# A cross-attention block feeding a maxout network on one core: scores and softmax with the tokens along the free dimension, VectorE's 32x32 transposes for the sums, one run of zero matmuls at the start, and the first tokens loaded in two halves of the heads

## The chip, the core and the metric

The kernel runs on one core of a Trainium2 chip. The metric is the device time of one execution in microseconds (us). The engines run in parallel, each with its own list of instructions in a fixed order, and meet through semaphores: PE (TensorE: matmuls and their weight loads), DVE (VectorE), ACT (ScalarE), POOL (GpSimd), and SP, which here only issues DMAs. PE writes to PSUM, which has eight banks; DVE and ACT copy out of PSUM into SBUF. POOL here works from SBUF to SBUF and issues the DMAs that change f32 into bf16 on the way.

## What is computed

```python
# attention, x: (8,8,512,64), state: (8,8,32,64)
scores = scale * x @ state^T          # (8,8,512,32)
a = softmax over the 32 states;       xread = a @ state
scores2 = scale * state @ x^T         # (8,8,32,512), the same numbers transposed
a2 = softmax over the 512 tokens;     sread = a2 @ x
y = concat([xread, sread], tokens)    # 8 batches of 512 + 32 rows, 8 heads x 64 = 512 columns
# maxout network on 4352 rows
h = max(y @ w1, y @ w2, y @ w3)       # 512 -> 768
out = h @ w_out                       # 768 -> 512
```

Both softmaxes come from one matrix of exponentials, summed over the states in one and over the tokens in the other.

## The kernel before, in words

Work is cut by batch. For a batch b the kernel does the following; the short names are those of its written schedule.

- `lx`, `pm`: load x[b] as bf16 by a POOL DMA, and permute it into `xn` (tokens on partitions). Batch 0 comes instead as f32 in one SP DMA (`x32`, 1 MB), behind the DMA of the state (`st32`, 512 KB).
- `xT` or `xb`: transpose `xn` into `xT`, by PE (16 transposes of 128x128 and two copies out of PSUM) for batches 0 to 2, by one SP DMA for the later ones.
- `S` (two halves of 256 tokens): scores `ps` with the tokens on the partitions (8 matmuls per half, each with 128x128 of `xT` as weights and 64 columns of the block-diagonal state `sbd` moving), the exponential `e` (ACT), the sum over the 32 states `den` and its reciprocal `rden` (DVE), and the product `a` (POOL).
- `aT` or `ab`: transpose `a` into `aT` (heads x states on the partitions), by PE for batches 0 to 2, by one SP DMA for the others.
- `R`: the state reads. 8 matmuls with `ones` sum `e` over the tokens, 16 matmuls multiply `xn` with `e`; DVE takes a 128x128 reciprocal (L279) and two products (L282) into `AT`.
- `M` (six units per batch): `M_sb`, the state of the batch already multiplied with the three weight matrices `W`. Eight matmuls per unit run side by side in tiles of 64 rows x 32 columns (`pm`); two copies of 128x384 bring them out.
- `u` (18 per batch, as block m = 0..5 and matrix i = 0..2): `pw`, two matmuls of 512 columns, `M_sb` against `aT`. Matrix 0 is copied out by ACT (`t`, L300), matrix 1 and 2 are folded in by DVE maxima against PSUM (L304, L306) into `ht`. The state rows of all batches form a ninth group that multiplies `AT` with `W` directly.
- `o` (8 per batch): `po`, `ht` against `wout`, three matmuls of 512 columns each; every second one ends with a copy by ACT and the output DMA from SP.

The order of the work is written out by hand: every engine runs its instructions in the order in which these strings name them. `OPENING` covers batch 0 and 1 and the attention of batch 2. `PERIOD` is used six times (the u of group g beside the o of the group before), `LAST` once. The groups run 0 to 6, then the state rows, then batch 7. `idle n` issues n matmuls of zeros into a bank that is not read; the opening has 9, 9 and 8 of them. POOL loads the weights in four pieces (`lw`, in columns of W), three DMAs each.

Where the profile says L106 or L109 that is the helper for all matmuls or transposes, and L101 or L103 the helper for all copies by ACT or by DVE and POOL; they are told apart by tile names.

Of the kernel before, what the change touches and what calls it, by code (L numbers as in the profile page):

```python
# [8 lines left out]
F32 = mybir.dt.float32  # L9
# [17 lines left out]

OPENING = """
id, idle 9, sel, idle 9, pm 0 0 a, pm 0 1 v, lx 1, xT 0 0 v, lw 2 4, pm 1 1 v, pm 1 0 v,
xT 0 1 a, idle 8, lw 1 2, lw 0 1, S 0 0 g, S 0 1 g, xT 1 1 a, xT 1 0 a, R 0, lw 4 6,  # L30
S 1 1 g, aT 0 0 a, M 0 2 va, aT 0 1 v, S 1 0 g, M 0 3 aa, M 1 3 av, M 1 2 aa, M 2 1 vv,
u 0 3 0, u 0 3 1, M 0 1 aa, u 0 2 0, M 1 1 va, aT 1 - v, u 0 2 1, M 0 0 aa, R 1, u 0 1 0,
lx 3, u 1 1 0, u 0 2 2, u 0 0 0, u 1 1 1, M 0 5 aa, M 0 4 aa, lx 2, u 0 1 1, u 0 3 2, lo,
u 1 3 0, u 0 0 1, u 0 5 0, M 1 0 va, pm 2 - g, u 1 3 1, u 1 1 2, u 0 4 0, M 2 2 aa,
u 1 3 2, lx 4, u 0 5 1, pm 3 - g, u 1 0 0, M 2 5 aa, M 1 5 aa, xb 3, u 0 1 2, u 0 5 2,
u 1 2 0, xT 2 1 v, u 0 4 1, u 0 0 2, u 1 5 0, u 0 4 2, xT 2 0 a, u 1 0 1, S 2 1 g,
o 0 0 0 v, M 1 4 aa, M 2 3 aa, o 0 0 1 v, u 1 2 1, o 0 1 0 v, S 2 0 g, u 1 5 1, u 1 2 2,
o 0 1 1 a, o 0 2 0 v, o 0 2 1 a, M 2 0 aa, M 2 4 aa, aT 2 - v, u 1 4 0, u 1 0 2, u 1 5 2,
o 0 3 0 v, o 0 3 1 a, u 1 4 1, u 1 4 2, R 2
# [4 lines left out]
u u u P L S S o o u M M m o u u o u u u o u u o X u M m m R u o u u u o u u  # L44
"""
LAST = """
u u u u u u M M u u u S u o u o u u M u u R u u M o u o S M L o M P o o X o
# [4 lines left out]
def kernel(  # L52
# [9 lines left out]
):  # L62

# [22 lines left out]
    xnp = ctx.enter_context(tc.tile_pool(name="xnp", bufs=3))  # L86
    att2 = ctx.enter_context(tc.tile_pool(name="att2", bufs=2))
    tmpp = ctx.enter_context(tc.tile_pool(name="tmpp", bufs=4))
# [19 lines left out]
    def tr(out_ap, in_ap):  # L108
# [6 lines left out]

    st32 = res.tile([128, Ns // 2, D], F32, name="st32")
    nc.sync.dma_start(
        out=st32.rearrange("p n d -> p (n d)"),
        in_=state.rearrange("b h (q n) d -> (b h q) (n d)", q=2))

    x32 = res.tile([128, H, J, D], F32, name="x32")
    nc.sync.dma_start(out=x32.rearrange("p h j d -> p h (j d)"),
                      in_=x[0].rearrange("h (p j) d -> p h (j d)", j=J))
    zeros = const.tile([128, 512], BF16, name="zeros")
    nc.vector.memset(zeros, 0.0)  # L125
    sbd = res.tile([128, B, HP, 2, Ns], BF16, name="sbd")
# [14 lines left out]
    def load_w(m0, m1):  # L141
        c = slice(m0 * 128, m1 * 128)
        for i in range(3):
            nc.gpsimd.dma_start(out=W[:, i, :, c], in_=w_v[i][:, :, c])  # L144
# [307 lines left out]
```

The softmax here doesn't subtract the row's maximum and nothing guards it: scores larger than these inputs give would overflow.

## Time and profile before

| what | value |
|---|---|
| median of 13 runs | 160.4 us (159.81 to 160.61) |
| the profiled execution's own time | 160.61 us |
| its span (first to last instruction) | 158.8 us |
| PE busy | 149.8 us, 94% |
| DVE, ACT, POOL busy | 112.0 (71%), 94.6 (60%), 44.2 (28%) us |
| last matmul ends | 155.40 us |
| one repeat of `PERIOD` (from one `S S` to the next) | 15.66 us (49.74 to 65.41, 65.41 to 81.07, ...) |

A line of groups names a source line, an engine, an operation and its output and inputs; then how often it ran, the busy time that the group covered, and the mean duration of one in nanoseconds. Matmuls overlap in the pipeline, so a mean duration of 380 ns does not mean that one can start only every 380 ns: the chain of waits shows two `pw` matmuls in 0.43 us. The chain of waits is followed back from the last instruction, and each of its lines gives a start, a length and what ran or was waited for.

### The profile page before, as it was taken

The page shows a single profiled execution, that of the slowest core. Times are in us where ns is not written, and L with a number is a line of the kernel's source. Part 1 is how long each engine was busy: PE and PEld are TensorE (multiplying, and loading weights), DVE is VectorE, ACT ScalarE, POOL GpSimd, SP SyncE. Part 2 cuts the span into 40 slices and gives each one's busy share as a digit, 9 for nine tenths or more (in the row PEclk, how much of TensorE's full clock was granted, in tenths as well). Part 3 has the DMA queues.
Part 4 walks back from the last instruction along what each step waited for, and adds up shares of the span by engine and source line. Part 5 has one row for each costly group of instructions (what it writes and reads, how often), then busy time and mean ns, then how long its engine had stood idle before and what let it go on. Part 6 is the DMA issues. An engine that isn't in the chain of part 4 may idle for free.

```text
span 158.8 us, 3558 instructions
## 1 busy us (share of the span) xinstructions
PE 149.8 (94%) x1387; PEld 75.3 (47%) x1404; DVE 112.0 (71%) x200; ACT 94.6 (60%) x188; POOL 44.2 (28%) x48
## 2 busy tenths in 40 slices
PE   7858899999999999999999999999999999999991
PEld 2337453344445445444444444454444467754450
DVE  3356999978669879867896889688968834478601
ACT  3557979668464956595658566855676533344440
POOL 8915990092550740092009000400040000000000
PEclk9999999999999999999999999999999999999999
DMA  4999999979649589729981708270306033030253
GB/s 148 290 194 190 149 176 155 191 111 196 109 114 261 114 202 132 214 50 170 163 232 40 198 0 210 60 198 2 136 20 179 4 132 132 0 132 4 66 187 143
DMA packets 34400, 21.46 MB, mean 135 GB/s; under 512 B 19536, under 2 KB 31824, under 8 KB 34384
## 3 DMA queue, kind: packets, MB, share of 16 engines
q0 software_dynamic: 14400, 6.82, 34.0%
q1 hardware_dynamic: 19840, 14.29, 32.6%
q8 instruction: 11, 0.18, 0.4%
q10 hardware_dynamic: 144, 0.13, 0.2%
q14 instruction: 5, 0.04, 0.1%
HBM read 15.20 MB, written 8.91 MB: 152 GB/s over the span
## 4 chain that ended last, share of the span: by engine, by line
PE 85%; DMA 5%; DVE 3%; ACT 2%; issue 1%; POOL 1%; SPq 0%; DVEq 0%; POOLq 0%
PE pw L106 43%; PE po L106 28%; PE pm L106 6%; DMA x<-in_x_dram 5%; PE pr L106 4%; PE ps L106 2%; PE px L109 1%; DVE M_sb L103 1%; POOL a L246 1%; PE pz L106 1%; PE pa L109 1%; DVE den L242 1%; ACT M_sb L101 1%; ACT xn L101 1%; ACT e L238 0%
## 5 line engine op out<-in xcount | busy, mean ns | idle before, releaser
L106 PE MATMUL pw<-aT,M_sb 128*128 128x512 bf16 x288 | 71.9, 380 | 0.0
L106 PE MATMUL po<-wout,ht 128*128 128x512 bf16 (+1 forms) x194 | 51.1, 373 | 0.8
L304 DVE TENSOR_TENSOR t<-t,pw 128x512 bf16<-128x512 bf16 (+1 forms) x54 | 35.4, 655 | 19.1 <-PE pw L106 8.9
L300 ACT CAST t<-pw 128x512 bf16<-128x512 f32 (+1 forms) x54 | 30.6, 569 | 29.3 <-PE pw L106 28.9
L106 PEld LDWEIGHTS <-M_sb 128*128 128x128 bf16 x288 | 26.9, 98 | 30.9 <-issue 0.8
L306 DVE TENSOR_TENSOR ht<-t,pw 128x512 bf16<-128x512 bf16 (+1 forms) x54 | 35.2, 657 | 6.8 <-PE pw L106 3.0
L246 POOL TENSOR_TENSOR a<-e,rden 128x512 bf16<-128x512 bf16 x16 | 16.4, 1041 | 59.6 <-ACT e L238 36.3
L101 ACT CAST M_sb<-pm 128x384 bf16<-128x384 f32 x75 | 31.1, 509 | 1.3 <-PE pm L106 0.6
L101 ACT COPY o<-po 128x512 f32<-128x512 f32 x32 | 18.7, 585 | 18.6 <-PE po L106 16.1
L106 PEld LDWEIGHTS <-ht 128*128 128x128 bf16 x210 | 19.6, 98 | 21.3 <-issue 1.9
L103 POOL COPY xn<-x 128x2048 bf16<-128x2048 bf16 x6 | 11.3, 1887 | 8.2 <-DMA x<-in_x_dram 8.2
L106 PE MATMUL pm<-W,sbd 64*32 64x384 bf16 x384 | 12.4, 327 | 0.1
L242 DVE TENSOR_REDUCE den<-e 128x16 f32<-128x512 bf16 x16 | 10.6, 661 | 2.2 <-ACT e L238 2.1
L238 ACT ACTIVATE e<-ps 128x512 bf16<-128x512 f32 x16 | 9.0, 598 | 4.6 <-PE ps L106 4.6
L103 DVE CAST M_sb<-pm 128x384 bf16<-128x384 f32 x21 | 10.6, 534 | 0.0
L144 POOL DMA_DIRECT2D W<-in_moe_w_dram x12 | 9.0, 766 | 4.0 <-DMA x<-in_x_dram 3.3
L106 PE MATMUL pw<-AT,W 128*128 128x256 bf16 x72 | 9.2, 273 | 0.1
L106 PEld LDWEIGHTS <-sbd 64*32 64x32 bf16 x384 | 4.4, 90 | 9.3 <-issue 8.7
L106 PE MATMUL pz<-zeros 128*128 128x512 bf16 x25 | 7.5, 457 | 1.2 <-DVE zeros L125 1.2
L106 PEld LDWEIGHTS <-W 128*128 128x128 bf16 x72 | 7.0, 98 | 2.5
L279 DVE RECIPROCAL rd<-pr 128x128 f32<-128x128 f32 x8 | 7.6, 944 | 0.0
L153 POOL DMA_DIRECT2D x<-in_x_dram x7 | 6.6, 943 | 0.1
(39 smaller groups left out, 66.8 us busy)
## 6 DMA issues: line engine op xcount, KB each, us to landing
out_dram<-o SPq DMA_DIRECT2D x14, 512.0 KB, 2.9
x<-in_x_dram POOLq DMA_DIRECT2D x7, 512.0 KB, 7.5
W<-in_moe_w_dram POOLq DMA_DIRECT2D x6, 256.0 KB, 7.8
x<-in_x_dram SPq DMA_DIRECT2D x1, 1024.0 KB, 7.4
W<-in_moe_w_dram POOLq DMA_DIRECT2D x6, 128.0 KB, 10.8
wout<-in_moe_w_out_dram POOLq DMA_DIRECT2D x1, 768.0 KB, 12.8
out_dram<-o SPq DMA_DIRECT2D x3, 256.0 KB, 2.1
st<-in_state_dram SPq DMA_DIRECT2D x1, 512.0 KB, 3.7
```

What stands on the lines that cost most here:

```text
L101: nc.scalar.copy(out=o, in_=i)
L103: ENG[eng].tensor_copy(out=o, in_=i)
L106: nc.tensor.matmul(out_ap, lhsT, rhs, start=start, stop=stop, tile_position=pos)
L144: nc.gpsimd.dma_start(out=W[:, i, :, c], in_=w_v[i][:, :, c])
L153: nc.gpsimd.dma_start(out=x_sb[b].rearrange("p h j d -> p h (j d)"), in_=x[b].rearrange("h (p j) d -> p h (j d)", j=J))
L238: nc.scalar.activation(out=e.rearrange("p r n -> p (r n)"), in_=ps.rearrange("p j a hp n -> p (j a hp n)"), func=AF.Exp, scale=scale)
L242: nc.vector.reduce_sum(out=den, in_=e, axis=AX.X)
L246: ENG[eng].tensor_mul(out=a_of(b)[:, 2 * h:2 * h + 2].rearrange("p j a hp n -> p (j a hp) n"), in0=e, in1=rden.unsqueeze(2).to_broadcast(( ...
L279: nc.vector.reciprocal(out=rd, in_=pd.rearrange("p (hp n) -> p hp n", hp=HP))
L300: nc.scalar.copy(out=t[:, :nn], in_=pw[:, :nn])
L304: nc.vector.tensor_max(t[:, :nn], t0[:, :nn], pw[:, :nn])
L306: nc.vector.tensor_max(ht[:, m, :nn], tiles["t", g, m][:, :nn], pw[:, :nn])
```

## The change

Scores and softmax are turned round. Now the state is the stationary operand and xT the moving one, so heads x states lie on the partitions and the 512 tokens along the free dimension.

- `S` is one step per batch: eight matmuls of 512 columns in tiles of 64 rows x 32 columns, as `M` has them, into two banks (one per parity of the head). `sbd` is replaced by the smaller `sT`. The two exponentials also give the sums over the tokens (`accum_out`, tile `den2`).
- `D` gives `aT` directly: a DVE reduction that transposes its input in blocks of 32x32 (L282 of the new file), a reciprocal, a DVE transpose of the broadcast reciprocals into `rb` (L288), and a product of `e` and `rb` on POOL or DVE (L290). The transposes `aT` and `ab` of the old kernel are gone.
- `E` scales `e` by the reciprocal of `den2` into `a2T` (two operations of 128x512); `eb` transposes that by one SP DMA into `a2` for every batch; `R` is then 16 matmuls and two plain copies. The matmuls with `ones`, the 128x128 reciprocal and the two products are gone.
- Some `u` of matrix 1 (written `w`) are copied out of PSUM by ACT, and DVE takes the third maximum later, between SBUF tiles (L346).
- `idle 14` stands alone at the start; the runs of 9 and 8 later are gone.
- x[0] is loaded as two DMAs of four heads each, the first ahead of the state, the second behind it; it is permuted in quarters (`p0`), and `xT` is made by pairs of heads. POOL's first load waits for the first half (`hold`, a copy of one column).
- `M` lies in a pool of five buffers. `OPENING`, `PERIOD` and `LAST` are written anew.

```diff
 OPENING = """
-id, idle 9, sel, idle 9, pm 0 0 a, pm 0 1 v, lx 1, xT 0 0 v, lw 2 4, pm 1 1 v, pm 1 0 v,
-xT 0 1 a, idle 8, lw 1 2, lw 0 1, S 0 0 g, S 0 1 g, xT 1 1 a, xT 1 0 a, R 0, lw 4 6,
-S 1 1 g, aT 0 0 a, M 0 2 va, aT 0 1 v, S 1 0 g, M 0 3 aa, M 1 3 av, M 1 2 aa, M 2 1 vv,
-u 0 3 0, u 0 3 1, M 0 1 aa, u 0 2 0, M 1 1 va, aT 1 - v, u 0 2 1, M 0 0 aa, R 1, u 0 1 0,
...
+id, idle 14, p0 0 0 a, lx 1, lw 4 6, lw 1 2, pm 1 0 g, ca 1 v, lw 0 1, p0 0 1 a,
+p0 1 0 a, ca 0 v, xT 0 0 a, sel, p0 1 1 v, xT 0 1 v, pm 1 1 v, S 0, xT 1 1 a, D 0 1 g,
+xT 1 0 a, S 1, lw 2 4, lx 2, D 0 0 v, M 0 5 av, M 0 4 aa, M 1 4 va, D 1 0 g, M 0 1 va,
+D 1 1 g, M 1 5 aa, lx 3, u 0 4 0, u 0 4 1, lo, u 0 5 0, u 0 1 0, u 0 5 1, M 1 1 aa,
...
 PERIOD = """
-u u u P L S S o o u M M m o u u o u u u o u u o X u M m m R u o u u u o u u
+w w P w B u e w O o m M M o w w L X o o o w O o D m m m u u u r u w w w u S u u
 LAST = """
-u u u u u u M M u u u S u o u o u u M u u R u u M o u o S M L o M P o o X o
+u w m u u w w d M u o O u u w M m u w w u L M u E u w B u S o R o o M P O O X O
...
+    def load_x32(k):
+        nc.sync.dma_start(
+            out=x32[:, 4 * k:4 * k + 4].rearrange("p h j d -> p h (j d)"),
+            in_=x[0, 4 * k:4 * k + 4].rearrange("h (p j) d -> p h (j d)", j=J))
...
+    def hold():
+        if not held:
+            held.append(const.tile([128, 1], F32, name="held"))
+            nc.gpsimd.tensor_copy(out=held[0], in_=x32[:, 0, 0, 0:1])
...
+    def scores(b):
+        ps = [bank([128, S], F32, "ps") for _ in range(2)]
+        for hp in range(HP):
+            for par in range(2):
+                r = slice(par * 64, par * 64 + 64)
+                mm(ps[par][hp * 32:(hp + 1) * 32, :], sT[r, b, hp, :], xT(b)[r, :, hp, :],
+                   True, True, pos=(par * 64, hp * 32))
+        den2 = tile_of("den2", b, att3, [128, 2], F32)
+        for par in range(2):
+            nc.scalar.activation(out=e_of(b)[:, par, :], in_=ps[par], func=AF.Exp, scale=scale,
+                                 accum_out=den2[:, par:par + 1])
+
+    def softmax_n(b, par, eng):
...
+        nc.vector.tensor_reduce(out=den, in_=e.rearrange("p (k n) -> p k n", n=32), axis=AX.X,
+                                op=mybir.AluOpType.add, apply_transpose=True)
...
+            nc.vector.reciprocal(out=rden, in_=den)
...
+        nc.vector.transpose(out=rb.rearrange("p (k n) -> p k n", n=32),
+                            in_=rden.unsqueeze(2).to_broadcast((128, k, 32)))
+        ENG[eng].tensor_mul(out=aT(b)[:, p, :].rearrange("p a t -> p (a t)"), in0=e, in1=rb)
+
+    def softmax_t(b, eng):
+        nc.vector.reciprocal(out=rden2, in_=tiles["den2", b])
+        for par in range(2):
+            i, o = e_of(b)[:, par, :], a2T(b)[:, par, :]
+            if eng == "a":
+                nc.scalar.activation(out=o, in_=i, func=AF.Copy, scale=rden2[:, par:par + 1])
+            else:
+                ENG[eng].tensor_scalar_mul(out=o, in0=i, scalar1=rden2[:, par:par + 1])
+
+    def a2_crossbar(b):
         nc.sync.dma_start_transpose(
...
+    def state_reads(b, eng):
+        pr = bank([128, HP, 2, Ns], F32, "pr")
         for hp in range(HP):
             for j in range(J):
-                mm(psr[:, hp, :, :], x_nat(b)[:, j, 2 * hp:2 * hp + 2, :], e[:, j, :, hp, :],
-                   False, hp == HP - 1 and j == J - 1)
-        rd = att2.tile([128, HP, Ns], F32, tag="rd", name="rd")
-        nc.vector.reciprocal(out=rd, in_=pd.rearrange("p (hp n) -> p hp n", hp=HP))
+                mm(pr[:, hp, :, :], x_nat(b)[:, j, 2 * hp:2 * hp + 2, :], a2(b)[:, :, j, hp, :],
+                   hp == 0 and j == 0, hp == HP - 1 and j == J - 1)
         for par in range(2):
-            nc.vector.tensor_mul(out=AT[r, :, b * Ns:(b + 1) * Ns],
-                                 in0=psr[r, :, par, :], in1=rd[r])
+            copy(eng, AT[r, :, b * Ns:(b + 1) * Ns], pr[r, :, par, :])
...
         elif i == 1:
+            if eng:
+                nc.scalar.copy(out=t[:, :nn], in_=pw[:, :nn])
+                tiles["late", g, m] = eng
+            else:
+                nc.vector.tensor_max(t[:, :nn], tiles["t", g, m, 0][:, :nn], pw[:, :nn])
         else:
+            nc.vector.tensor_max(h, tiles["t", g, m, 0 if late else 1][:, :nn], pw[:, :nn])
+            if late:
+                ENG[late].tensor_max(h, h, tiles["t", g, m, 1][:, :nn])
```

## The prediction

> **What bounds the kernel now.** I read the page's busy shares and slices first, then the chain of waits, then the groups by form, last the stages.
>
> ```profile
> span 158.8 us, 3558 instructions
> PE 149.8 (94%) x1387; PEld 75.3 (47%) x1404; DVE 112.0 (71%) x200; ACT 94.6 (60%) x188; POOL 44.2 (28%) x48
> PE   7858899999999999999999999999999999999991
> PE 85%; DMA 5%; DVE 3%; ACT 2%; issue 1%; POOL 1%; SPq 0%; DVEq 0%; POOLq 0%
> ```
>
> PE is full from the fifth slice on. The chain says what it is full of:
>
> ```profile
> 1.20 7.42 DMA x<-in_x_dram
> 8.64 1.05 ACT xn L101
> 10.81 1.73 PE pz L106 x8
> ...
> 14.57 0.73 POOL a L246
> 16.67 0.40 PE pa L109 x4
> 21.59 0.43 PE pw L106 x2
> ...
> 65.41 0.47 PE ps L106 x16
> 65.87 1.29 PE po L106 x6
> 67.17 0.43 PE pw L106 x2
> 67.60 0.61 PE pm L106 x24
> ...
> 74.97 0.92 PE pr L106 x24
> ```
>
> Up to about 22 us the chain hops between engines: x must land, then softmax runs, and no `u` can start without `aT`. From there it is PE back to back. The prices of PE's work per issue: `pw` and `po` 0.216 us, a unit of `pm` 0.20 us, `S S` 0.47, `R` 0.92 us per batch.
>
> ```profile
> L304 DVE TENSOR_TENSOR t<-t,pw 128x512 bf16<-128x512 bf16 x48 | 32.8, 684 | 12.6 <-ACT t L300 6.0 <-PE pw L106 3.5 <-ACT M_sb L101 2.3
> L300 ACT CAST t<-pw 128x512 bf16<-128x512 f32 x48 | 28.4, 593 | 25.2 <-PE pw L106 25.1
> L242 DVE TENSOR_REDUCE den<-e 128x16 f32<-128x512 bf16 x16 | 10.6, 661 | 2.2 <-ACT e L238 2.1
> L279 DVE RECIPROCAL rd<-pr 128x128 f32<-128x128 f32 x8 | 7.6, 944 | 0.0
> 64.10:79.70 15.60, 15.50 (x148) 7.39 (x148) 12.55 (x23) 10.29 (x21) 4.76 (x4) 1.00 0.77 152
> q0 software_dynamic: 2347, 0.96, 153.2%
> ```
>
> The fifth line is one period: PE 15.50 of 15.60 us, DVE 12.55, ACT 10.29. The last is POOL's DMA queue from 10 to 15 us: 0.96 MB in 5 us, so 0.19 MB per us.
>
> **After the opening, the period.** Cut the old execution where the opening's last `R` ends, 48.45 us; PE's last matmul ends at 155.40. Between lie R and S of five batches. R loses its 8 matmuls with `ones`; its other 16 have the shape of 16 `ps`, 0.47 us, so R saves 0.45, five times 2.25. The new S is 8 matmuls in `pm`'s tiles, 0.20 x 512/384 = 0.27, and alone between other shapes a `pm` unit takes 0.28 instead of 0.20, so 0.35: it saves 0.12. One more S than before has gone into the opening, so 4 x 0.12 + 0.47 = 0.95. Together 3.2 us, PE's period 15.1.
>
> This counts only if DVE and ACT follow. DVE per new period: 8 maxima against PSUM x 0.685 = 5.5; 4 copies of M, 2.0; 4 maxima SBUF to SBUF; one reciprocal 128x32 (0.35, between 0.253 for 16 and 0.944 for 128 elements) and one of 2 (0.2); two scalings; the transposing reduction and the transpose, 1024 columns each. The last kinds are in no row. An SBUF maximum lies between the 0.29 of the product with 128 columns (L282) and 0.685; I take 0.4, so 1.6, and for a scaling 0.3 (the 128x1024 copy of `xn` takes 0.52). The reduction of 1024: twice L242, 1.3. The transpose: below, the `xn` copy's 0.52; above, the 6.2 ns per element that L279 and L245 give, 6.3 us; I take 1.4, one pass at the rate of L242, its nearest neighbour in operand and shape. Sum 12.9 of 15.1: covered, as 12.55 of 15.6 was. If the cover went, each further us would cost five.
>
> ACT: 10 casts of pw 5.9, 4 of po 2.3, 8 of M 3.3 (0.415 back to back), 2 of AT 0.6, 2 exponentials 1.2 plus 0 to 0.25 each for the sums: 13.5 of 15.1, up from 10.3. It runs late by up to 2 us where five M copies follow four casts, and catches up under the `o`s; eight banks hold that. I allow 0.7 us in all for the places where they don't. POOL (product 2.1, permute 1.9, load 0.9) has room. SP gets a transpose for `a2` in place of the one for `aT`, 1.45 us of its queue, with the outputs queued behind it; a `PERIOD` leaves some 14 units between `X` and `r`, about 5 us, against 3.7 to landing. At nothing, on that cover.
>
> The end is as before: the two last `o` halves of the state group, 1.3 us, hide the last two maxima (0.685 + 0.4); after PE 3.4 us remain (155.40 to 158.8).
>
> **The opening.** x's first half leads the SP queue. The state's 512 KB took from 0.74 to 4.43, so this half lands near 4.5. The POOL copy that waits for it holds x[1] and all weights back by some 3 us. In the packet records, though, POOL's queue moved nothing before 6.3 us, although x[1] was issued at 1.44, and came to its full rate when x32's packets ended, 8.5; so the hold moves little. I cost it at nothing; from above it is those 3 us, from below -1, as x32 would land undisturbed at 7.3. Second half at 7.3 to 8.6, say 8.2. Then: quarter permute 0.55, eight transposes 0.5, copy 0.7, S 0.4, two exponentials 1.3, reduction 0.7, reciprocal 0.25, transpose 0.7, second half of the same on DVE 1.7 with its product 0.4: `aT` at 15.5 to 15.9. The old chain had the state of `aT` at 18.7 (copies after `pa`); its PE transposes and their copies are gone.
>
> But M must be there too: POOL's order x[1] (0.52 MB), W 4-6 (0.79), W 1-2 (0.39), from 8.5 at 0.19 MB/us with 0.25 MB already moved, puts W 1-2 at about 16.5 to 17.3, and `M 0 1` stands on PE before the first `u`. First `pw` near 17.9 (old: 18.74, but unbroken only from 22.0).
>
> From 15.8 DVE has, up to the end of the opening, 22 maxima on PSUM 15.1, four transposed half softmaxes 6.5, 9 copies of M 4.5, 2 of xT 1.4, the rest 1.7: 29.2, so not before 45.0. PE from 17.9: 36 u 15.6, 8 o 5.2, 13 M 3.0, S and R 2.1, 16 transposes 0.9: 26.8, not before 44.7. Two engines so equally full wait for each other now and then; I take 46.0, against 48.45.
>
> [...] Nine zero matmuls took 3.73 us at the start, eight later ones 1.90; the old runs of 9 and 8 filled waits, the new kernel has from 6 to 17 us only short pieces with gaps of up to 1.6 us by my chain. The old trace has a gap of 1.7 us (8.06 to 9.74) and no slowing after it. [...]
>
> [...]
>
> **Sum.** Opening 46.0 - 48.45 = -2.45; period -3.2 + 0.7: -4.95 on the profiled execution's own 160.61, so 155.7. That execution was 0.2 above the median of 160.4; predicted 155.4.
>
> **The rivals.**
> - *The opening goes better* (transposes at the `xn` copy's rate, four halves x 0.44 less on DVE, 1.8 us, and W one us earlier): 43 us at its end, 152.4.
> - *PE's clock falls in the opening* and PE restarts slowly once or twice: nine in 3.73 us against 0.216 each is half speed, so 1.9 us lost per restart: 157 to 159. For it: the fillers are gone. Against: the gaps are short.
> - *ACT becomes the bound of the period*: if the sums of the exponentials and unoverlapped M copies (0.509) cost it 1.3 more, 14.8 plus bursts, period 15.6: five times 0.5, 158. For it: 90% full in strict order.
> - *Slower: the 32x32 operations take several passes.* Say reduction and transpose of a batch cost P together, 2.7 in my sum. DVE's rest is 10.2, so it bounds the period from P = 4.9; the opening gets 4 halves, 2(P - 2.7). Time = 155.4 + 5(P - 4.9) + 2(P - 2.7), equal to before at P = 5.0, 1.9 times what I take; at 6.3 + 1.3 it is 179. For it: L279 shows that DVE can need 6 ns per element. Against: L242 needs 1.3.
> - *The change does not do what it says*: no; the matmuls with `ones` and the transposes of `a` are out of PE's list.
>
> **How the numbers follow.** Forecast, with its own range 153 to 158 (opening's end 44 to 48.5): 0.59. Better opening 0.11. Clock 0.09. ACT 0.07. Slow transposes 0.14, of which 0.01 ends within 0.2% of before, about what runs of this kernel can tell from no change; another 0.01 of ACT's case does. So faster 0.85, same 0.02, slower 0.13. The range takes in the better opening's and the clock's prices and leaves out the slow transposes: 151.8 to 159.8.
>
> **What would show it.** L282 and L288 near 1.3 and 1.4 us for 1024 columns; `pr` only as x16; `ps` 32x512 in 0.35; spacing of `S` to `S` 15.1; first `pw` at 17 to 19; DVE nearly unbroken from 16 to 45. Wrong it would be through transposes above 2.5 us each, a first `pw` after 21, or PE idle in the periods behind ACT.

## The result, and the profile after

The changed kernel takes 161.88 us (median; 161.53 to 162.74) where the kernel before takes 160.39 beside it: a ratio of 1.0117, 95% interval 1.0095 to 1.0139. It is slower by 1.2%; the forecast was 155.4, with a range that ended at 159.8. The profiled execution took 161.80 us, with a span of 160.0. Some executions of a kernel run in a slower state; the ratios here and below leave those out, the medians keep them.

The page of the changed kernel; the digits are tenths in 40 slices, the last line the chain of waits by engine:

```profile
span 160.0 us, 3311 instructions
PE 145.3 (91%) x1219; PEld 69.1 (43%) x1240; DVE 113.3 (71%) x202; ACT 107.1 (67%) x239; POOL 52.2 (33%) x48
PE   7934699999999996999999999999999999999990
PEclk9995569999999999999999999999999999999999
PE 70%; DMA 14%; DVE 5%; issue 4%; POOL 3%; ACT 1%; DVEq 0%
```

PE has less to do, as forecast (149.8 to 145.3 us, though the records at half clock lengthen the latter: three `pw` take 1.46 us from 19.85, ten take 2.32 from 77.03), and yet is last to end. Three things are new: slices 3 and 4 (8 to 16 us) have PE busy for only 30 and 40%, the granted clock is at half in slices 4 to 6, and the sixteenth slice has a hole. Transfers hold 14% of the chain instead of 5%. The chain names two of them:

```profile
9.16 9.78 DMA W<-in_moe_w_dram
18.95 0.14 issue
19.08 0.84 PE pm L114 x15
...
52.03 9.18 DMA a<-a2T
61.21 0.05 issue
61.26 0.64 PE pr L114 x16
```

W 1-2 lands at 18.95, and PE's `M 0 1` and the first `pw` wait for it; `a2`'s transpose of the first period takes 9.2 us from issue to landing, and the first `r` waits.

Stages (length, then busy time of PE, PE's weight loads, DVE, ACT and POOL, granted clock, DMA share, GB/s): the stretch before the clock fell, the stretch at half clock, and three periods from one `S` to the next.

```profile
9.10:12.50 3.40, 1.05 (x13) 0.28 (x10) 0.69 (x1) 1.60 (x5) 0.84 (x2) 1.00 1.32 170
12.50:22.80 10.30, 7.22 (x71) 3.36 (x73) 9.81 (x18) 6.68 (x15) 9.07 (x11) 0.50 1.53 172
63.98:79.28 15.30, 15.20 (x131) 6.71 (x132) 12.54 (x21) 12.26 (x28) 4.29 (x3) 1.00 0.94 155
79.28:95.17 15.89, 15.35 (x130) 6.77 (x132) 13.75 (x23) 12.27 (x28) 4.50 (x3) 1.00 0.96 150
95.17:111.07 15.90, 15.42 (x132) 6.78 (x133) 13.66 (x25) 12.27 (x28) 2.12 (x1) 1.00 0.55 117
```

The period should have gone from 15.66 to 15.1. One is 15.30 long; the next two are 15.9, longer than before, with DVE 1.2 us busier for the same work. The timeline (start, length) shows where that comes from:

```profile
77.06 1.88 POOL L111 COPY xn<-x 128x2048 bf16<-128x2048 bf16 x1
77.28 1.94 DVE L346 TENSOR_TENSOR ht<-ht,t 128x512 bf16<-128x512 bf16 x1
```

L346 is the new maximum from SBUF to SBUF. It takes 0.42 us by itself and 1.94 us here, beside POOL's permute copy. The new operations themselves came in at their price (busy us, mean ns; the 546 of L346 has two such collisions in it, and the last line, from the best kernel further down, has none):

```profile
L288 DVE STREAM_TRANSPOSE rb<-rden 128x1024 bf16<-128x1024 bf16 x5 | 6.2, 1246 | 0.5
L282 DVE TRANSPOSE_TENSOR_REDUCE den<-e 128x32 f32<-128x1024 bf16 x5 | 6.2, 1238 | 0.0
L346 DVE TENSOR_TENSOR ht<-ht,t 128x512 bf16<-128x512 bf16 x25 | 13.7, 546 | 2.5
L346 DVE TENSOR_TENSOR ht<-ht,t 128x512 bf16<-128x512 bf16 x20 | 8.5, 425 | 2.4 <-ACT M L109 0.5
```

Laid out along the span, before against after (us):

| stretch | before | after | forecast | measured |
|---|---|---|---|---|
| start to the end of the opening's last `R` | 48.45 | 48.18 | -2.45 | -0.27 |
| from there to PE's last matmul | 106.95 | 107.73 | -2.5 | +0.78 |
| from there to the end of the span | 3.4 | 4.1 | 0 | +0.7 |

### The profile page after: what moved, and what is told of

Its sections match the earlier page's. It is cut to its first block, busy times and chain, and to the rows that moved or that the text cites. A ratio compares the mean times of both kernels' runs of the same rounds, so it can differ in the third digit from the quotient of the medians.

```text
span 160.0 us, 3311 instructions
## 1 busy us (share of the span) xinstructions
PE 145.3 (91%) x1219; PEld 69.1 (43%) x1240; DVE 113.3 (71%) x202; ACT 107.1 (67%) x239; POOL 52.2 (33%) x48
## 4 chain that ended last, share of the span: by engine, by line
PE 70%; DMA 14%; DVE 5%; issue 4%; POOL 3%; ACT 1%; DVEq 0%
PE pw L114 37%; PE po L114 26%; DMA W<-in_moe_w_dram 6%; DMA a<-a2T 6%; PE pm L114 4%; POOL W L162 2%; DMA x<-in_x_dram 2%; PE pr L114 2%; DVE M L111 2%; DVE ht L344 2%; DVE t L340 1%; ACT o L109 1%; POOL x L172 1%; ACT M L109 1%; PE ps L114 1%
## 5 line engine op out<-in xcount | busy, mean ns | idle before, releaser
L114 PE MATMUL pw<-aT,M 128*128 128x512 bf16 x275 | 68.9, 385 | 1.5 <-DVE ht L344 0.4
L114 PEld LDWEIGHTS <-M 128*128 128x128 bf16 x288 | 26.8, 99 | 34.9 <-issue 7.1
L332 ACT CAST t<-pw 128x512 bf16<-128x512 f32 (+1 forms) x54 | 30.9, 575 | 16.2 <-PE pw L114 13.9
L290 POOL TENSOR_TENSOR aT<-e,rb 128x512 bf16<-128x512 bf16 (+1 forms) x10 | 16.4, 1639 | 65.1 <-DVE rb L288 59.3
L109 ACT CAST M<-pm 128x384 bf16<-128x384 f32 x67 | 27.7, 502 | 1.4 <-PE pm L114 1.1
L340 DVE TENSOR_TENSOR t<-t,pw 128x512 bf16<-128x512 bf16 (+1 forms) x25 | 16.3, 660 | 2.4 <-PE pw L114 1.5
L111 DVE CAST M<-pm 128x384 bf16<-128x384 f32 x29 | 14.9, 550 | 3.4 <-PE pm L114 3.1
L337 ACT CAST t<-pw 128x512 bf16<-128x512 f32 (+1 forms) x29 | 16.3, 561 | 1.0 <-PE pw L114 0.7
L346 DVE TENSOR_TENSOR ht<-ht,t 128x512 bf16<-128x512 bf16 (+1 forms) x29 | 14.8, 511 | 2.9
L111 POOL COPY xn<-x 128x2048 bf16<-128x2048 bf16 (+1 forms) x7 | 12.8, 1835 | 2.9 <-DMA x<-in_x_dram 2.9
L114 PE MATMUL pm<-W,sT 64*32 64x384 bf16 x384 | 12.5, 346 | 1.2 <-DMA W<-in_moe_w_dram 1.0
L288 DVE STREAM_TRANSPOSE rb<-rden 128x512 bf16<-128x512 bf16 (+1 forms) x11 | 10.5, 955 | 0.8
L282 DVE TRANSPOSE_TENSOR_REDUCE den<-e 128x16 f32<-128x512 bf16 (+1 forms) x11 | 10.4, 941 | 0.0
```

Source lines behind the costliest of these rows:

```text
L109: nc.scalar.copy(out=o, in_=i)
L111: ENG[eng].tensor_copy(out=o, in_=i)
L114: nc.tensor.matmul(out_ap, lhsT, rhs, start=start, stop=stop, tile_position=pos)
L282: nc.vector.tensor_reduce(out=den, in_=e.rearrange("p (k n) -> p k n", n=32), axis=AX.X, op=mybir.AluOpType.add, apply_transpose=True)
L288: nc.vector.transpose(out=rb.rearrange("p (k n) -> p k n", n=32), in_=rden.unsqueeze(2).to_broadcast((128, k, 32)))
L290: ENG[eng].tensor_mul(out=aT(b)[:, p, :].rearrange("p a t -> p (a t)"), in0=e, in1=rb)
```

## The experiments

The theory after reading the two traces: the change does what it says, and its saving is eaten at five places, each of which can be taken away without touching the change: the half clock and `M 0 1` in the opening, `a2`'s late transpose, the collision of L346 with POOL's copy, and a longer end. The rival: the wait only moves to the next late thing, so that no edit of this kind helps. Ratios are to the kernel before, measured beside each kernel.

### One loss at a time

**Zero matmuls where PE is sparse** (the fillers), to hold the clock:

```diff
-pm 1 1 v, S 0, xT 1 1 a, D 0 1 g, xT 1 0 a, S 1, ... D 1 0 g, M 0 1 va,
+pm 1 1 v, S 0, idle 10, xT 1 1 a, D 0 1 g, xT 1 0 a, idle 4, S 1, ... D 1 0 g, idle 4, M 0 1 va,
```

> Theory: the changed kernel loses time in four places that do not depend on each other. In the opening PE's clock is granted at half from 12.5 to 22.8 us, because PE has only short pieces of work once the later zero matmuls are gone; this run puts zero matmuls back into three waits of PE (10 behind the scores of batch 0, 4 ahead of those of batch 1, 4 ahead of the first unit of M that waits for weights) and leaves all else. The clock should then stay at 1.0 through the opening; the first u still waits for the weights that land at 18.95, so it starts at 19.6 to 19.9, but the seven u up to 22.8 us take 0.43 us each instead of 0.86: about 1.4 us less, 160.4 us. Rival: the opening is bound by DVE's queue as the prediction had it; then the clock returns, the opening still ends near 48.2, and the time stays within 0.3 us of 161.9.

161.5 us, ratio 1.011 (1.0069 to 1.015). The clock stays (page), but PE then waits (us in total, times, longest) for the same W and for `a2`:

```profile
PEclk9999999999999999999999999999999999999999
PE pm L114 <- DMA W<-in_moe_w_dram: 1.8, 2, 1.5
PE pr L114 <- DMA a<-a2T: 1.4, 2, 0.9
```

First `pw` at 20.38 instead of 19.85; the opening's fourth `S` starts at 44.91 instead of 45.45. Half a microsecond won there, 0.2 us by the end of PE's work (155.66 against 155.89), and the end after PE is longer by 1.15 us (5.26 against 4.11): one issue of an output on SP takes 1.69 us instead of 0.43.

**`M 0 1` later** (behind `u 0 5 1` instead of ahead of `D 1 1`):

```diff
-D 1 0 g, M 0 1 va, D 1 1 g, M 1 5 aa, lx 3, u 0 4 0, u 0 4 1, lo, u 0 5 0, u 0 1 0, u 0 5 1, M 1 1 aa,
+D 1 0 g, D 1 1 g, M 1 5 aa, lx 3, u 0 4 0, u 0 4 1, lo, u 0 5 0, u 0 5 1, M 0 1 va, u 0 1 0, M 1 1 aa,
```

> One unit of M (batch 0, block 1), the first that needs the weights of blocks 1 and 2, stands ahead of the first u on PE and waited for their DMA until 18.95 us. Here it stands four u later, behind u 0 5 1; nothing else moves. Theory: the first u starts when M of block 4 is copied out, near 18.3, still at half clock; about 0.8 us less, 161.1 us. Rival (DVE's queue binds the opening): PE starts earlier and waits later for DVE, time unchanged at 161.9.

162.39 us, ratio 1.0156 (1.0122 to 1.019). The first `pw` came at 19.35, 0.5 earlier, but PE then waited 1.5 us for DVE's copy of M, which stood behind `D 1 1`, and 0.7 for ACT's; the fourth `S` started at 46.06, later than in the changed kernel. A miss.

**The collision.** The eighth `u` of the period (block 2, matrix 1) is folded in by DVE against PSUM, so the SBUF maximum that ran beside POOL's copy is gone:

```diff
-w w P w B u e w O o m M M o w w L X o o o w O o D m m m u u u r u w w w u S u u
+w w P w B u e w O o m M M o w w L X o o o u O o D m m m u u u r u w w w u S u u
```

> In each period the third maximum of block 2 (L346, two SBUF inputs) falls on POOL's permute copy of the next x and took 1.94 us instead of 0.42 in the second and third period (77.3 and 93.2 us); PE's next stretch was 0.6 to 0.8 us longer both times. Here this one u is folded in against PSUM by DVE, so this L346 does not exist; the other three per period stay. Theory: no L346 over 0.5 us, two times 0.7 less, 160.5 us, although DVE has 0.27 us more work per period. Rival: the periods lose time because ACT runs late, not by the collision; then ACT having 0.6 us less per period would help in all five periods alike, and the periods without a collision (the last two) would be shorter too.

162.18 us, ratio 1.0157 (1.0115 to 1.0199). No L346 is above 0.43 us any more, and from `S` to `S` the third and fourth stretch are 15.65 and 15.43 instead of 15.89 and 15.90. The time did not fall: the second stretch is 16.94 instead of 15.30, with a new wait for `a2`. In all the weight loads of PE (PEld) waited for it as follows (us in total, times, longest), against 1.8 us, once, in the changed kernel:

```profile
PEld L114 <- DMA a<-a2T: 3.2, 3, 2.0
```

**`r` later**, to cover `a2`'s late landing:

```diff
-... o D m m m u u u r u w w w u S u u
+... o D m m m u u u u w w w r u S u u
```

> In the first period PE stood still at 59.8 to 61.2 us for the transposed a2 of batch 3, whose DMA took 9.2 us to land. Here the state reads stand four u later in the period. Theory: the wait is covered, 1.4 us less in the first period and nothing elsewhere, 160.5 us. Rival: the DMA's lateness only moves the wait to the next thing that DVE or ACT bring late, and less than 0.5 us is won.

161.47 us, ratio 1.0108 (1.0065 to 1.0151): within the error of the changed kernel, with 1.1 us of PE's waiting for `a2` left of 1.3 (1.6 of 1.8 for its weight loads). What stood between was too little. Its profiled execution, at 163.0 us, is the longest of its six, and its mean granted clock was 0.957, against 0.966 in the changed kernel's.

**The end.** Near the end SP runs nine waits for DMA semaphores, one behind the other. In the changed kernel they start from 156.78 to 159.11; the last output lands at 158.34, and the wait for it is the fourth, so that five follow it. Before, they start from 156.23 to 157.87; the last output lands at 157.76, and the wait for it is the eighth. Four more transfers in mid-run are to move that place:

```diff
-                nc.sync.dma_start(out=rows[j - 1:j + 1].rearrange("j p f -> p j f"), in_=o)
+                if g < 2:
+                    nc.sync.dma_start(out=rows[j - 1], in_=o[:, 0, :])
+                    nc.sync.dma_start(out=rows[j], in_=o[:, 1, :])
+                else:
+                    nc.sync.dma_start(out=rows[j - 1:j + 1].rearrange("j p f -> p j f"), in_=o)
```

> The changed kernel, with the outputs of the groups 0 and 1 written to memory one block of rows at a time, so that four more transfers go through SP's queue in the middle of the run, where nothing waits for them, and the last transfer's semaphore stands later in SP's final list of waits, as it does in the kernel before. Theory 1 (the end costs 0.6 us more than before because of that place in the list): from the landing of the last output to the end of the span 1.66 us becomes about 1.05, as before; the time of after falls by 0.6, ratio to the kernel before about 1.008. Theory 2 (the longer end belongs to the work, not to the list): it stays at 1.6 and the ratio at 1.012 or above, by the cost of four more transfers.

161.19 us, ratio 1.007 (1.003 to 1.0109). From PE's last matmul to the end 3.3 us, against 4.1 in the changed kernel and 3.5 before. It is the one loss that comes off by itself, since nothing follows it; the time falls by about as much, though the interval still overlaps that of the changed kernel.

**`a2`'s bounce (its transpose by DMA) ahead of the next x's on SP**:

```diff
-w w P w B u e w O o m M M o w w L X o o o w O o D m m m u u u r u w w w u S u u
+w w w e X P B u w O o m M M o w w L o o o w O o D m m m u u u r u w w w u S u u
```

> The changed kernel with one move in the period: the bounce of a2 (its store and its transposing load) is issued on SP ahead of the transposing load of the next x, not behind it. Theory 1 (a2's transpose lands 9.2 us after its issue in the first period because it queues behind the 256-byte packets of x's, which POOL's load of x slows): it lands within 4 to 5 us, the first r waits for nothing (1.3 to 1.5 us of PE's idle time go), ratio 1.002 to 1.005. Theory 2 (a single removal only shows the next late thing, as in the runs before): the next S or the next xT then is late by as much, and the ratio stays at 1.010 to 1.013.

161.35 us, ratio 1.0092 (1.0057 to 1.0128). `a2`'s transpose (x1, median us to landing) goes from 9.2 in the changed kernel

```profile
a<-a2T SPq DMA_TRANSPOSE x1, 9.2
```

to 4.6 here,

```profile
a<-a2T SPq DMA_TRANSPOSE x1, 4.6
```

and the wait is gone: 17.08 us from the opening's last `S` to the next, instead of 18.53. But the three following periods are all 15.9, each with the collision, where the changed kernel had one of 15.30, and the opening's fourth `S` came at 45.78. The gain at the end of PE's work is 0.5 us.

**The opening as a whole**: the fillers, and `M 0 1` later with both copies on ACT.

```diff
-p0 1 1 v, xT 0 1 v, pm 1 1 v, S 0, xT 1 1 a, D 0 1 g, xT 1 0 a, S 1, ... D 1 0 g, M 0 1 va,
-D 1 1 g, M 1 5 aa, lx 3, u 0 4 0, u 0 4 1, lo, u 0 5 0, u 0 1 0, u 0 5 1, M 1 1 aa,
+p0 1 1 v, xT 0 1 v, pm 1 1 v, S 0, idle 10, xT 1 1 a, D 0 1 g, xT 1 0 a, idle 4, S 1, ... D 1 0 g,
+D 1 1 g, M 1 5 aa, lx 3, u 0 4 0, u 0 4 1, lo, u 0 5 0, u 0 5 1, M 0 1 aa, u 0 1 0, M 1 1 aa,
```

> The changed kernel with zero matmuls after S 0 and before S 1, so that the clock is not taken away, and with W 1-2's consumer later: M 0 1 comes after the first three gate passes and both its copies go to ACT. Theory 1 (the opening's loss is the half clock and M 0 1 in front of a busy VectorE, together): clock 1.0 from 7 us on, the fourth S of the opening starts at 44.0 to 44.5 instead of 45.45, the time falls by 1 to 1.5, ratio 1.002 to 1.006. Theory 2 (an earlier end of the opening is given back at the first r, since a2 is late): the start of the period is earlier but the wait ahead of r grows by as much, ratio 1.009 to 1.013.

162.11 us, ratio 1.0115 (1.0064 to 1.0165). PE does what theory 1 says and a little more: the fourth `S` at 43.86. Then theory 2 takes over: the next `S` is only 1.5 us earlier (62.48), after 1.4 us of PE's waiting for `a2` (2.1 for its weight loads). And again one issue of an output on SP is long, 1.96 us instead of 0.43: the last copies wait for their buffer, and the end after PE's last matmul is 5.5 us long.

### All of them

> The three edits above in one kernel (the outputs of two groups in single blocks, a2's bounce ahead of the next x's, the opening with the filled clock and the later M 0 1), and the permute copy of POOL one step away from the max reductions of VectorE (a w of the period becomes a u). Theory 1 (the losses stand behind one another: each one taken away alone shows the next, all taken away show the gain that the change was to bring): opening -1 to -1.5, a2 -1.3, collisions -1.2, end -0.6, together 3 to 4.5 us less than after, 157.0 to 158.5 us on a chip where before has 160.2; ratio 0.98 to 0.99. Theory 2 (VectorE and POOL, or the transfers, are the bound of the period, and no order of the work makes it shorter): the periods stay at 15.9 and the ratio at or above 1.0.

159.66 us, ratio 0.996 (0.9928 to 0.9992): below the kernel before. The kernel has the edit to the end, `a2`'s bounce first, the opening as a whole and the `u` in place of the `w`. The edit to the collision is worded loosely in the expectation: POOL's copy doesn't move, the maximum beside it is gone. By the ratios that is 2.5 us less than the changed kernel; the four edits by themselves had given -0.8 (the end), -0.4 (`a2`), 0 (the opening) and +0.6 us (the collision). So the losses did stand behind one another, and theory 1 is right in kind. It is short of its 3 to 4.5 us; two losses that it did not have are left, a wait of 1.0 us for `a2` at the end of the opening and the long issue on SP.

Then the parts were taken out again, one at a time.

**Without the edit to the collision** (`u` back to `w`):

> The kernel with all edits, less one: the step of the period that was turned from w to u is a w again, so that POOL's permute copy falls on the max reductions of VectorE. Theory 1 (in the whole, where nothing else is late, the collision costs what its slowed max reductions cost PE): the 2nd and 3rd period take 15.9 instead of 15.4, the time is 0.8 to 1.3 us above the kernel with all edits, ratio to the kernel before about 1.003. Theory 2 (the collision is hidden, as the run with this edit alone, which gained nothing, can be read): the same time as the kernel with all edits, ratio 0.996.

160.38 us, ratio 1.0011 (0.9979 to 1.0043). The collision is back in the timeline,

```profile
76.19 1.88 POOL L111 COPY xn<-x 128x2048 bf16<-128x2048 bf16 x1
76.42 1.94 DVE L346 TENSOR_TENSOR ht<-ht,t 128x512 bf16<-128x512 bf16 x1
78.28 0.68 DVE L340 TENSOR_TENSOR t<-t,pw 128x512 bf16<-128x512 bf16 x1
```

all three periods are 15.9 instead of 15.43, and PE ends 1.9 us later (0.6 of that already in the opening). The edit that gained nothing alone is worth 1.4 us of PE's time here. By the ratios it is 0.8 us, with intervals that overlap a little; the end after PE's work is 0.9 us shorter in this run, where the long issue on SP took only 1.07 us.

**Without the edit to `a2`'s order**:

> The kernel with all edits, less one: the order of the bounces on SP in the period is that of after (the next x's transpose ahead of a2's). Theory 1: a2's transpose of the first period lands 8 to 9 us after its issue, the first read waits 1.3 to 1.5 us, and the time is 1.0 to 1.5 us above the kernel with all edits, ratio about 1.004. Theory 2 (with the earlier opening a2 is in time anyway): the same time as the kernel with all edits.

160.36 us, ratio 1.0005 (0.997 to 1.0041), but PE's work ends at the same time as with all edits (153.1 against 153.2), and PE itself stands still for `a2` for 0.3 us instead of 1.0. On PE's side theory 2 holds: with the earlier opening this edit is worth nothing. The times of the two kernels differ by 0.7 us with intervals that overlap, and the traces do not say from what: the two profiled executions differ by 0.2.

**Without the fillers, and the read `R 2` last.** `R 2` waited 1.0 us for `a2`, so it was put behind 0.9 us of other work:

```diff
-R 2 a, R 1 a, u 1 3 2
+R 1 a, u 1 3 2, R 2 a
```

> The kernel with all edits, less the zero matmuls after S 0 and before S 1. Two things are asked of it. First, what the half clock costs where nothing else is late: theory 1, PE is at half clock for 10.24 us again and the fourth S of the opening starts 0.5 to 1.0 us later than 43.54, which now reaches the end of PE's work (153.5 to 154.0 instead of 152.9); theory 2, the opening waits for W's loads and copies at that time, and the start of that S moves by less than 0.3. Second, whether the long issue on SP among the last outputs (1.69 to 1.96 us, in four of the five kernels with all the fillers, in none without) goes with the fillers: if it does, the end after PE's last matmul falls from 5.1 to about 4 us, and the time is within 0.5 us of the kernel with all edits, ratio 0.993 to 0.999; if it stays, the ratio is 1.000.

> The kernel with all edits, and at the end of the opening the read R 2 behind R 1 and the last step of up, so that 0.9 us of PE's work stand before the read that waits 1.0 us for a2[2]'s transpose. Theory 1 (the wait is covered and nothing else is late): PE's end 0.9 us earlier, ratio 0.990 to 0.991. Theory 2 (the gain goes into the next late thing, as when x[4]'s load was moved): the next S or r waits by as much more, ratio 0.996.

> Both of the edits before: no fillers, and R 2 last. If the two are worth what theory 1 of each says, the end of PE's work is at 152.5 to 153.0, the end after it about 4 us, ratio 0.988 to 0.992; if the long issue on SP stays or the gain of R 2 moves on, ratio 0.996 or above.

Fillers off: 159.88 us, ratio 0.9991 (0.9962 to 1.0021). `R 2` last: 159.33, ratio 0.9932 (0.99 to 0.9965). Both: 159.49, ratio 0.9953 (0.9932 to 0.9975). With `R 2` last, the opening's fourth `S` starts (first number) as follows, first with fillers, then without:

```profile
43.53 0.40 PE L114 MATMUL ps<-xT,sT 64*32 64x512 bf16 x8
46.08 0.40 PE L114 MATMUL ps<-xT,sT 64*32 64x512 bf16 x8
```

PE's work ends at 152.11 and at 154.56. So the half clock, worth 0.5 us at that `S` when its fall was the only thing mended, costs 2.5 us of PE's time once the other things are. That is more than theory 1 gave it. With `R 2` as it was, the fillers are worth 2.5 us at that `S` and 1.4 at the end of PE's work (153.18 against 154.58), since the wait for `a2` takes back the rest; and without fillers `R 2` last gains nothing there (154.58 and 154.56). In the time of the kernel little of this arrives: 159.66 against 159.88, and 159.33 against 159.49, with overlapping intervals, because the end after PE's work is 1.1 to 1.3 us longer with fillers. Without the fillers the page has the same fall as the changed kernel (fillers off, `R 2` as it was):

```profile
PEclk9995569999999999999999999999999999999999
```

The kernel with all edits, fillers and `R 2` last has the lowest median of all, 0.9 us below the kernel before; it is called the best kernel below, though the one without fillers is not told from it. Its page, and three of its periods:

```profile
span 156.8 us, 3360 instructions
PE 147.0 (94%) x1254; PEld 69.1 (44%) x1254; DVE 109.1 (70%) x201; ACT 104.4 (67%) x234; POOL 52.2 (33%) x48
```

```profile
60.85:76.28 15.43, 15.43 (x133) 6.71 (x132) 12.29 (x23) 11.77 (x27) 4.84 (x4) 1.00 0.80 154
76.28:91.72 15.44, 15.44 (x134) 6.71 (x134) 12.30 (x23) 11.77 (x27) 4.85 (x4) 1.00 0.77 155
91.72:107.15 15.43, 15.43 (x134) 6.70 (x133) 12.38 (x23) 11.77 (x27) 3.92 (x2) 1.00 0.45 121
```

PE is busy all of each period by the profile, and the period is 15.43, 0.23 shorter than before; not 0.56, as forecast. A little is hidden in it: the same work of PE took 15.30 in the changed kernel's first period, and here the third `pw` behind `pr` starts 0.36 us after the second instead of 0.22. So the change is worth at most 0.36 us in a period. This execution took 158.56 us by itself, 0.8 below its median. Its end is still long; the chain there (start, length):

```profile
148.39 1.63 SPq L386
150.01 0.04 issue
150.06 1.72 DMA out_dram<-o
...
152.07 0.58 ACT o L109
152.66 0.28 ACT oh L109
```

An issue of 1.63 us on SP, a late landing, a late buffer, a late copy: 4.7 us from PE's last matmul to the end, against 3.5 without fillers. Of the eight changed kernels with fillers, seven have an issue of 1.34 to 1.96 us among the last outputs and the eighth one of 1.07 us; of the eight without, none has one above 0.5 us there. (The expectation's count of this is off; these are the numbers.) The traces also show what stands beside it. The queue that the profile calls "instruction" moved ten loads of 16 KB in the best kernel, and nine in the same without fillers; from the two pages:

```profile
q8 instruction: 10, 0.16, 0.4%
q8 instruction: 9, 0.15, 0.4%
```

The pages of four more kernels with fillers (e1_fill, e7_open, e8_all, e9_lx4) have ten of these loads too, and those of the changed kernel and of e13_nofill nine. In the changed kernel the ninth comes at 131.73 us; in the best kernel the tenth ends at 149.66, among the last outputs, and the long issue beside it at 150.01. That the fillers cost their time at the end through this one load more is not shown: no run moves that load, and in the kernel before, which has eleven, the last of them (146.23 to 147.12) has issues of only 0.34 and 0.58 us beside it.

**A third output buffer**, to take the copy out of that chain (with `lx 4` moved as in the next run):

> The same as the run before it, with a third buffer for the output tiles. In the kernel with all edits one issue on SP took 1.76 us instead of 0.43 among the last outputs, the last group's copies waited for their buffer, and from the last matmul to the end there were 5.1 us against 3.6 where no issue was long. Theory 1 (the long issue costs because the buffer comes back late): with a third buffer the copies of ACT don't wait, and the end is 0.7 to 1.0 us shorter. Theory 2 (the last transfers are behind SP's late issues, whatever the buffers): no change, within 0.3 us of the run before it.

Median 160.54 us, 158.07 to 163.05; ratio 0.9921 (0.9877 to 0.9966). The median is of all twelve executions and the ratio of only six of them; the times scatter more than those of the other kernels, and the profiled execution's mean granted clock was 0.987, against 0.997 in the next run's. By the ratio this is 0.8 us less than the next run, as theory 1 has it, but the intervals overlap, and from its last matmul to the end the profiled execution took 4.6 us, against 4.4 in the next run. Inconclusive.

**x[4]'s load behind `a2`'s bounce**, in the kernel with all edits (`R 2` as it was):

```diff
-u 0 2 1, u 1 4 1, lx 4, ... eb 2, D 2 0 g,
+u 0 2 1, u 1 4 1, ... eb 2, D 2 0 g, lx 4,
```

> The kernel with all edits, and the load of x[4] moved in the opening from its place ahead of group 0's first outputs to behind the bounce of a2[2]. In the kernel with all edits SP's queue moved nothing from 26 to 42 us, while POOL's queue moved W, wout and x[4]; a2[2]'s transpose, issued at 38.14, landed at 46.3, and PE waited 1.0 to 1.5 us for it at the first two reads of the state. Theory 1 (a transpose lands behind the bytes that POOL's queue was given before it): without x[4] ahead of it a2[2] lands at 42 to 44, the wait goes, the time falls by 1.0 to 1.5 us against the kernel with all edits, ratio to the kernel before about 0.988. Theory 2 (the transposes are slow by their own packets, whatever runs beside them): a2[2] lands at 46 as before and the ratio stays at 0.996. Rival for the gain: x[4] lands too late for POOL's copy of it at 45.0, POOL is late by 1 to 2 us in the first period, and the wait moves to S.

The expectation's first figure was misread: the records of packets start 10.4 us ahead of the span, so that the stretch named is 15.6 to 31.6 in the span's time. Up to 27.77 SP's queue had nothing to move there; then `a2[0]`'s transpose was issued, and from 28 to 31 it moved no packet while POOL's queue moved 807. For `a2[2]` the two microseconds from 38 to 40 show it. `a2[2]`'s transpose is issued at 38.14 in the kernel with all edits (packets, MB, share of 16 engines; then us to landing):

```profile
q0 software_dynamic: 556, 0.28, 114.1%
q1 hardware_dynamic: 30, 0.00, 2.1%
...
a<-a2T SPq DMA_TRANSPOSE x1, 8.1
```

and at 38.17 where x[4] is not ahead of it:

```profile
q1 hardware_dynamic: 769, 0.19, 132.9%
...
a<-a2T SPq DMA_TRANSPOSE x1, 3.3
```

SP's queue moves 30 packets in these two microseconds beside 556 of POOL's queue, and 769 when x[4] is not there. It is not always so sharp: in the best kernel the same stretch has 288 packets of SP's queue beside 412 of POOL's, and the transpose lands after 8.0 us too. Theory 1 of the mechanism fits these two runs (8.1 us to landing against 3.3), and the rival for the gain is right: x[4] lands late, POOL is late, x's transpose is late, and the wait reappears before `S`:

```profile
PE ps L114 <- DMA xT<-xn: 2.2, 1, 2.2
```

160.07 us, ratio 0.9974 (0.9947 to 1.0002): no better than with all edits.

## Why the prediction was wrong, point by point

- **"The change does not do what it says: no"**: right. The matmuls and transposes are gone, and the 32x32 operations cost 1.24 and 1.25 us for 1024 columns, against 1.3 and 1.4 in the sum. The rival that needed 5.0 us for the pair (here 2.5) is out. L288 takes 0.712 us for 512 columns and 1.246 for 1024, which is 0.18 us once and 1.04 ns per column.
- **DVE and ACT follow the period**: right. 12.5 of 15.30 us for DVE (12.9 forecast) and 12.3 for ACT (13.5), in the changed kernel's first period. The rival "ACT becomes the bound" is out. So the loss lay in order and in collisions, and in the size of PE's own saving, not in the busy time of DVE or ACT.
- **"so R saves 0.45" and, of S, "it saves 0.12"**: mis-sized. The old `R` alone took 0.82 us, not 0.92, and the new 0.47: 0.35 saved. The new `S` takes 0.34 us and the change between its 64x32 tiles and the 128x128 ones 0.09 more (`ps` starts 0.30 us after the last `pw`, at 63.98, where one `pw` starts 0.22 after another): 0.43 against 0.465, 0.03 saved. Together 5 x 0.35 + 4 x 0.03 + 0.47 = 2.3, not 3.2. By this PE's floor is 15.28 for a period, not 15.1; the shortest measured is 15.30.
- **For an SBUF maximum "I take 0.4", and POOL "has room"**: both right as busy times (0.425 us; POOL 33%), and wrong together. The step priced each engine alone and never asked what POOL runs at the moment of the new maximum. Two of the collisions, 1.94 us instead of 0.42, lengthen one period each by 0.47 (15.9 against 15.43 without them): 0.95 us. In the opening, too, DVE's product ran beside POOL's and took three times its forecast:

```profile
16.04 1.20 POOL L290 TENSOR_TENSOR aT<-e,rb 128x512 bf16<-128x512 bf16 x1
16.30 1.23 DVE L290 TENSOR_TENSOR aT<-e,rb 128x512 bf16<-128x512 bf16 x1
```

  Both of these have two inputs in SBUF, like L346 with its 0.42 against 1.94 us. The maxima of the kernel before have one input in PSUM, and there is no such loss in its trace; L304 takes 0.69 us inside POOL's copy, against a median of 0.686:

```profile
54.78 1.88 POOL L103 COPY xn<-x 128x2048 bf16<-128x2048 bf16 x1
55.96 0.69 DVE L304 TENSOR_TENSOR t<-t,pw 128x512 bf16<-128x512 bf16 x1 [0.63 <-ACT t L300]
```

  So no row of the kernel before shows what a maximum or product with both inputs in SBUF costs VectorE beside POOL's copy.
- **"At nothing, on that cover"** (5 us between `X` and `r` against 3.7 to landing): the step that failed most cleanly. The landing took 9.2 us, with x's transpose ahead of it on SP and POOL's load of x beside both (4.6 us when it went ahead of x's): 1.3 us of PE's idle time. The 3.7 was the median of five landings in the kernel before, which has one of 7.5 among them.
- **The opening, 46.0**: PE could nearly do it (the last read ends at 46.8 in the best kernel), but not in the order given. W 1-2 landed at 18.95, not 16.5 to 17.3, while W 0-1, issued behind it at 13.8, shared the queue's rate (2.06 MB moved by then where 1.7 were needed); and `M 0 1`, which needs it, stands ahead of all `u`. The first `pw` came at 19.85, not 17.9.
- **"Against: the gaps are short"**: wrong, and the dearest single mistake of the opening. The rival of the falling clock had 0.09. The prediction's chain had gaps of up to 1.6 us; the longest was 2.50 us (10.54 to 13.04), and the clock fell in the midst of it, at 12.53, after 3.42 us in which PE was busy for 1.04. It stayed at half until 22.77, for 10.24 us. In the kernel before, the clock stayed at full through the gap of 1.68 us (8.06 to 9.74), with PE busy for 1.74 of the 3.42 us around it. The two stretches (length, PE's busy time, ...; each is a third of the 10.24 us long, by the author's choice):

```profile
9.11:12.53 3.42, 1.04 (x13) 0.27 (x10) 0.69 (x1) 1.59 (x5) 0.83 (x2) 1.00 1.32 170
7.90:11.32 3.42, 1.74 (x21) 1.23 (x21) 1.64 (x4) 1.52 (x2) 0.32 (x1) 1.00 1.44 194
```

  Whether the length of the gap or PE's small share decides, these two do not show. Over the three thirds of the stretch at half clock PE was busy for 1.93, 2.07 and 3.19 us, and the clock came back after the last. The profiled executions of the eight changed kernels without the fillers have a mean granted clock of 0.957 to 0.968, those of the eight with them 0.987 to 0.999. The loss was 2.5 us of PE's time (with the other losses mended); the rival had 1.9 for one fall.
- **"The end is as before"**: wrong by 0.7 us, for a reason that no part of the change names: four more transfers on SP (42 instead of 38), so that the last one is the fourth and not the eighth of SP's nine waits at the end. With four more still (46) the end took 3.3 us, against 3.5 before.
- **The sum**: -0.27 in the opening instead of -2.45. After it -2.3 + 1.3 + 0.95 is -0.05, which leaves 0.8 of the measured +0.78 to all the rest, against an allowance of 0.7 for bursts; no run takes that apart. +0.7 at the end. The sign is wrong because terms that were set at nothing (the clock, W 0-1 beside W 1-2, `a2`, the collisions, the end) came to some 5 us, against a saving of 5.

What the prediction lacked in method is one thing. Its rivals were single mechanisms on busy time. No term asked what comes late: each term "at nothing" named a cover, and none named what else wants that cover at that moment.

## What to carry to other kernels

When a change moves work between engines, check the new operation against what the other engines run at that instant, and not only against their busy shares (here a maximum of 0.42 us took 1.94 beside POOL's copy). When one mended loss gains nothing, do not discard it: mend the next ones too, and test it by taking it out of the whole. A transfer's time to landing changed here with what was issued around it (`a2`'s transpose took 9.2 or 4.6 us in the first period, and 8.1 or 3.3 in the opening), so read it at the place where the change puts it. And when PE becomes sparse, look at its busy time around a gap and not only at the gap's length: here the clock fell with 1.04 us busy of 3.42 and a gap of 2.50, and stayed with 1.74 and a gap of 1.68.

## What was not expected of the hardware

- PE's granted clock halved at 12.53 us in the changed kernel, with no gap longer than 2.50 us and PE busy for 1.04 of the 3.42 us before, and stayed at half for 10.24 us. In the kernel before, it stayed at full with 1.74 of 3.42 us and a gap of 1.68.
- A VectorE maximum with two SBUF inputs took 4.6 times as long (1.94 against 0.42 us) beside a GpSimd copy in the changed kernel, and ended 0.3 us behind it (79.22 against 78.94).
- SP's queue, with a transpose to move, moved 30 packets in 2 us while POOL's queue moved 556 (all edits), and 769 when that queue moved none (x[4] behind `a2`'s bounce).
- The sum that comes with an exponential costs ACT a second instruction, 16 of them in the changed kernel, of 0.21 us each.
- One DMA issue on SP took 1.07 to 1.96 us instead of 0.43, near the end, in eight of eight changed kernels with more zero matmuls and in none of eight without. In the best kernel it took 1.63 us and ended 0.35 us after a tenth 16 KB load of the queue called "instruction" (150.01 against 149.66).
